# First batch: another order on VectorE and TensorE from the second scores on, and weights in pieces of 2, 2, 3, 2 and 3 blocks

## Chip, cores and metric

The kernel runs on one core of a Trainium2 chip. The metric is the device time of one launch in microseconds, as a median of runs; the profile shows one execution of the same program.

## What is computed

For q, k and v of shape (8 batches, 8 heads, 576 positions, 64), heads 0 to 3 attend to the last 32 positions and heads 4 to 7 to every 32nd position. The attention output, as 4608 tokens of 512 channels, goes through a bilinear feed-forward network with 1536 hidden channels.

```python
mask_local = (rel >= 0) & (rel < 32)
mask_strided = (rel >= 0) & (pos[None, :] % 32 == pos[:, None] % 32)
attn = softmax(where(mask, q @ k.T / 8, -1e9))
x = (attn @ v).transpose(0, 2, 1, 3).reshape(4608, 512)
out = ((x @ w_a) * (x @ w_b)) @ w_out
```

Inputs and output are float32; the kernel casts to bf16 while it loads.

## The kernel before, in words

**Stages.** Attention of batch 0 is done first, in a prologue. Then the feed-forward network runs in nine stages of 512 tokens, each with 12 hidden blocks of 128 (`ffn_ab`) and four output steps (`ffn_y`, L768). The attention of the batches 1 to 7 is spread between these stages' steps (the tables `STEPS` and `LATER`). All instructions are issued under a manual schedule: each engine works in the order in which the program names them.

**Units of attention.** A head pair c (0 and 1 local, 2 and 3 strided) has two halves, so a batch has eight units u = 0 to 7 with c = u // 2. In the prologue these are single steps, named in the string `ORDER`:

- `Tkcp`, `Tqcp`: transposes of keys or queries of pair c on TensorE (L287, L290, L296) into a PSUM buffer `tp`, of which there are two, used in turn; `Tkce` (VectorE, L307) and `Tqce` (ScalarE, L311) copy them out.
- `Sup`: scores on TensorE into `st`, of which there is one (L379, L385); `Sux`: exp on ScalarE (L393); `Sum`: the mask as a bitwise and on VectorE (L403), for local units only. Strided units of batch 0 get their mask from a matmul inside `Sup` (L379).
- `Vup`: p times v on TensorE (L442, L444) into `o`, of which there are two; `Vur`, `Vun`: reciprocal and normalization on VectorE (L450, L465).
- `Xcp`, `Xce`: the normalized output is transposed on TensorE (L511) and copied to `xT` on ScalarE (L523). `Xcp` takes a `tp` buffer too.
- `*n`: n filler matmuls of 224 columns (`spin`, L154), whose result nobody reads.
- `C0`, `C1`: casts of the first pieces that came as float32 (L834, L838). `M` and `G0` to `G2` make the masks; `G2` is a small matmul (L149) and, on VectorE, `mask_s` (L150).
- `F0A` to `F1c`: the first two hidden blocks of the feed-forward network, in parts (L581). `Z` zeroes a query buffer on ScalarE.

**Weights.** `load_w(c)` (L252) brings the hidden blocks `WCH[c]` to `WCH[c+1] - 1` of w_a and of w_b, one transfer each, from float32 in HBM to bf16 in SBUF. A row that lies together is 128 columns for each block: 512, 768 or 1024 bytes of bf16 for two, three or four blocks. The calls stand in step `G1`, on GpSimd's queue, before and between the loads for batch 1 (`load_qk`, L197; `load_vs`, L238). `load_wo` (L255) follows later on the same queue, in four pieces of three blocks.

Of the kernel before, what the change touches and what calls it, by code (L numbers as in the profile page):

```python
# [22 lines left out]
PAD = 32  # L23
PW = 344
VW = 128
WCH = (0, 2, 5, 9, 12)
FAST_Y = (2, 3, 4, 5, 6, 7, 8)


# [1 line left out]
def kernel(  # L31
# [81 lines left out]
    def zero_qz(i, eng, parts=((0, 0), (0, 1), (1, 0), (1, 1))):  # L113
        for j, z in parts:
            t = qz_buf[i][j][z]
            if (i, j, z) == (0, 0, 0):
                t = t[:, 1]
            if eng is nc.scalar:
                nc.scalar.copy(t, spare[:, :1].unsqueeze(2).to_broadcast(list(t.shape)))
            else:  # L120
                eng.memset(t, 0.0)
# [8 lines left out]
    def mask_local2():  # L130
        nc.vector.tensor_copy(mask_l, msl.unsqueeze(1).to_broadcast([128, 4, LW]))

        nc.vector.memset(mask_l[:PAD, 0], 0)
# [4 lines left out]
    def mask_group(part):  # L138

        if part == 0:  # L140
            nc.scalar.copy(by4(nm_l[lo, :NP]), ident[lo, :NP // 4].unsqueeze(2).to_broadcast([32, NP // 4, 4]))
            nc.scalar.copy(by4(nm_l[up, :NP]), ident[up, 32:36].unsqueeze(1).to_broadcast([32, NP // 4, 4]))
            nc.scalar.copy(nm_l[64:], nm_l[:64])
        elif part == 1:
            nc.vector.tensor_scalar(nm_r[up], nm_l[up, :NP], 1.0, 8e9, op0=ALU.subtract, op1=ALU.mult)
            nc.vector.tensor_copy(nm_r[64:], nm_r[:64])
        else:
            mp = cur["misc"][:NP, 256:256 + NP]
            nc.tensor.matmul(mp, lhsT=nm_l[:, :NP], rhs=nm_r, start=True, stop=True)  # L149
            nc.vector.tensor_scalar(mask_s, mp, 0.0, -1.0, op0=ALU.is_equal, op1=ALU.mult)  # L150

    def spin(n):
        for _ in range(n):
            nc.tensor.matmul(cur["misc"][:, :224], lhsT=nc.const_aps.tensor(1.0, [128, 128], BF16),  # L154
                             rhs=nc.const_aps.tensor(1.0, [128, 224], BF16), start=True, stop=True)
# [31 lines left out]
    def load_qk(b, strided, heads=range(HL), names="kq"):  # L187
        for nm in names:
            src = {"k": k, "q": q}[nm]
            if b < FIRST_D:  # L190
                n, R, h0 = (NP, RS, HL) if strided else (96, RL, 0)
                w0 = {"k6": 0, "q6": 1536, "k8": 3072, "q8": 5120}[f"{nm}{R}"]
                if b not in shared:
                    shared[b] = nat.tile([128, FG * 5 * SW], BF16, tag="shared", name="shared")
                t = nats[b, nm, strided] = shared[b][:n, w0:w0 + HL * R * D].rearrange("p (h r d) -> p h r d", r=R, d=D)
                hs = slice(heads[0], heads[-1] + 1)
                nc.gpsimd.dma_start(out=t[:, hs], in_=src[b, h0:h0 + HL].rearrange("h (p r) d -> p h r d", r=R)[:, hs])  # L197
            elif strided:

                t = nat_s[nm]  # L200
                n = 32 if b == FIRST_D else YS
                for h in heads:
                    nc.gpsimd.dma_start(
                        out=t[32 * h:32 * h + n],
                        in_=bass.AP(tensor=src.tensor, offset=(b * H + HL + h) * S * D,
                                    ap=[[RS * D, n], [YS * RS * D, 3], [1, RS * D]]))
            else:
                if 0 in heads:
                    nats[b, nm, strided] = nat.tile([128, NY, D], BF16, tag=f"{nm}l", name=f"{nm}l")
                t = nats[b, nm, strided]  # L210
                for h in heads:
                    nc.gpsimd.dma_start(out=t[32 * h:32 * h + 32],  # L212
                                        in_=src[b, h].rearrange("(i y) d -> y i d", y=32))
            nats[b, nm, strided] = t
# [18 lines left out]
    def load_vs(b, heads=range(HL)):  # L233
        if b < FIRST_D:

            for z in range(2):
                t = blocks("k", z)
                nc.gpsimd.dma_start(out=t[:NP, :, :RS * D],  # L238
                                    in_=v[b, HL + 2 * z:HL + 2 * z + 2].rearrange("h (p r) d -> p h (r d)", r=RS))
                nats[b, "v", z] = t  # L240
            return
        for h in heads:
            nc.gpsimd.dma_start(out=vs_buf[b % 2][:, h, :, 0:D],  # L243
                                in_=v[b, HL + h].rearrange("(p r) d -> p r d", r=RS))
# [4 lines left out]
    def load_w(c):  # L249
        f = slice(128 * WCH[c], 128 * WCH[c + 1])  # L250
        for src, dst in ((moe_w_a, wa_sb), (moe_w_b, wb_sb)):
            nc.gpsimd.dma_start(out=dst[:, :, f], in_=src.rearrange("(ko ki) f -> ki ko f", ki=128)[:, :, f])  # L252
# [13 lines left out]
    def by_row(t):  # L266
        return t.rearrange("p (r h d) -> p h r d", h=2, d=D)
# [257 lines left out]
    def step_X(b, c):  # L525
# [6 lines left out]
            "Xp": lambda c: X_p(0, c), "Xe": lambda c: X_e(0, c)}  # L532

    ORDER = """
        G0 C0 Tk0p *2 Tq0p Tk0e Tq0e *5 Tk1p S1p M G1 Tq1p S1x Tk1e *4 Tq1e S0p S1m *7 G2 C1 S0x S3p Tk2p Tq2p Tk2e S3x Tq2e *3
        S2p S2x V1p S0m *2 V1r S3m V0p V0r V1n V0n *2 S4p Tk3p Tk3e S2m Tq3p S4x Tq3e *2 S5p S5x X0p X0e *3 V2p V2r V3p V2n
        V3r V3n S6p V4p V4r V4n S6x X1p V5p V5r S7p X1e V5n V6p S7x F0A V6r V7p V6n X2p X2e Z F1A F0B V7r V7n F1B X3p F0b X3e
        F1b F0c F1c""".split()


    STEPS = {1: {5.5: "Tk2", 6: "Tq2", 7: "S4 Tk3", 7.5: "S5", 8: "Tq3", 8.5: "V4", 9: "S6 V5 Pk0", 9.5: "S7 Pq0",
# [30 lines left out]
    def ab_mm(t, f, ab, kks, mid=None, first=0, last=KD - 1, ws=(0, 1)):  # L572
        n = min(TTOK, XR * S - TTOK * t % (XR * S))
        cuts = [(0, n)] + ([(n, TTOK - n)] if n < TTOK else [])
        for w, ps_ in [((wa_sb, wb_sb)[i], ab[i]) for i in ws]:
            if mid and ps_ is ab[1]:
                mid()
            for kk in kks:
                for c0, n in cuts:
                    x0 = (TTOK * t + c0) % (XR * S)  # L580
                    nc.tensor.matmul(ps_[:, c0:c0 + n], lhsT=w[:, kk, 128 * f:128 * (f + 1)], rhs=xT[:, kk, x0:x0 + n],  # L581
                                     start=(kk == first and c0 == 0), stop=(kk == last and c0 == cuts[-1][0]))
# [214 lines left out]
    with tc.manual_schedule(engines={ENG.PE, ENG.SP, ENG.Pool, ENG.DVE, ENG.Activation}):  # L797
# [30 lines left out]
        for nm in ORDER:  # L828
            if nm[0] == "*":
                spin(int(nm[1:]))  # L830
            elif nm == "C0":
                for x, cp, n in ((raw[0], nc.vector.tensor_copy, "k"), (raw[1], nc.scalar.copy, "q")):
                    t = nats[0, n, False][:, 0:2].rearrange("p h r d -> p (h r d)")
                    cp(by_row(t), x[:96].rearrange("p (h r d) -> p h r d", h=2, d=D))  # L834
                    paired[0, n, 0] = t.rearrange("p (r m) -> p r m", r=RL)
            elif nm == "C1":
                for p in (slice(PAD, 64), slice(64, 128)):
                    nc.vector.tensor_copy(vl_buf[0][p, 0, 0:D], raw[2][p, :D])  # L838
            elif nm == "M":
                mask_local2()  # L840
            elif nm[0] == "G":
                mask_group(int(nm[1]))
                if nm == "G1":
                    load_vs(0)
                    for c in range(2):
                        load_w(c)
                    load_w(2)
                    load_qk(1, True, (0, 1))
                    load_qk(1, True, (2, 3))
                    load_vs(1)  # L850
                    load_w(3)
                    load_qk(1, False)
            elif nm == "Z":
                zero_qz(1, nc.scalar, ((0, 0),))
            elif nm[0] == "F":
                f = int(nm[1])
                if nm[2] == "A":
                    if f == 1:
                        ab = pst.tile([128, 2, 512], F32, tag="st", name="ab")
                        first[f] = [ab[:, 0], ab[:, 1]]  # L860
                    else:
                        first[f] = [psum4["misc"].tile([128, 512], F32, tag="misc", name="ab")]
                elif nm == "F0B":
                    first[f].append(psum4["o"].tile([128, 512], F32, tag="o", name="ab"))
                ab_mm(0, f, first[f], {"A": (0, 1), "B": (0, 1), "b": (2,), "c": (3,)}[nm[2]],
                      ws={"A": (0,), "B": (1,)}.get(nm[2], (0, 1)))
            else:
                PART[nm[:-2] + nm[-1]](int(nm[-2]))
# [101 lines left out]
```

## Time and profile before

| | |
|---|---|
| median of 6 runs | 328.82 us (328.54 to 329.35) |
| profiled execution | 328.54 us, of which the span is 326.4 |
| TensorE busy | 319.5 us, 98% of the span |
| VectorE, ScalarE, GpSimd busy | 81%, 62%, 54% |
| granted TensorE clock | 1.00 throughout |
| DMA | 37.50 MB in 98869 packets; software queue 64.4% of 16 engines' span |

The span is the time from the first to the last instruction. An engine's busy share is an average over the whole span; where a stage differs, the chain of waits, the timeline and the windows show it. In the software queue's figures several packets overlap on one DMA engine, so a share can pass 100% within a window. Start times are microseconds from the start of the span.

### The profile page before, as it was taken

What the parts mean: (1) busy time and instruction counts of PE and PEld (TensorE: products, weight loads), DVE (VectorE), ACT (ScalarE), POOL (GpSimd) and SP (SyncE); (2) the same over time, 40 slices, a digit from 0 to 9 for tenths busy, and PEclk for the clock granted to TensorE, in tenths of its full rate; (3) what the DMA queues carried; (4) which work ended last, traced back from release to release, by engine and by line L of the source; (5) the groups of instructions that cost most, each with busy time, mean ns of one, the idle gap of its engine ahead of it and who ended that gap; (6) DMA issues with size and microseconds to landing.
All of it is one profiled execution on the core that took longest, in us unless ns stands there. A gap on an engine that the chain in (4) does not pass through costs nothing.

```text
span 326.4 us, 7644 instructions
## 1 busy us (share of the span) xinstructions
PE 319.5 (98%) x2788; PEld 206.1 (63%) x2820; DVE 265.7 (81%) x509; ACT 202.3 (62%) x329; POOL 177.0 (54%) x295
## 2 busy tenths in 40 slices
PE   8999999999999999999999999999999999999995
PEld 6754655455555587557999985569555954584474
DVE  6766888889778999999999999999877845647562
ACT  6764775478777765777677757775677643313321
POOL 8935838699866555875577557753312031232021
PEclk9999999999999999999999999999999999999999
DMA  9999999999999798799979999898024022004004
GB/s 154 151 203 201 203 185 190 161 177 134 134 207 122 91 100 78 76 222 120 84 73 190 147 86 76 152 189 84 20 63 129 2 67 64 0 2 129 1 2 129
DMA packets 98869, 37.50 MB, mean 115 GB/s; under 512 B 76688, under 2 KB 96016, under 8 KB 98832
## 3 DMA queue, kind: packets, MB, share of 16 engines
q0 software_dynamic: 85968, 19.48, 64.4%
q1 hardware_dynamic: 12576, 17.34, 18.3%
q8 instruction: 22, 0.36, 0.5%
q10 hardware_dynamic: 288, 0.20, 0.2%
q14 instruction: 15, 0.12, 0.1%
HBM read 39.51 MB, written 9.44 MB: 150 GB/s over the span
## 4 chain that ended last, share of the span: by engine, by line
PE 91%; DVE 3%; issue 2%; DMA 2%; POOL 1%; ACT 1%; POOLq 0%; DVEq 0%; ACTq 0%
PE mm L581 51%; PE mm L686 16%; PE mm L768 6%; PE st L385 4%; PE o L486 4%; PE misc L154 2%; DMA kl<-in_k_dram 2%; PE mm L714 2%; PE o L442 1%; PE ab L581 1%; PE tp L511 1%; PE tp L287 1%; PE end L714 1%; DVE xT L500 1%; PE tp L296 1%
## 5 line engine op out<-in xcount | busy, mean ns | idle before, releaser
L581 PE MATMUL mm<-xT,wb_sb 128*128 128x512 bf16 (+1 forms) x465 | 109.1, 357 | 0.2
L581 PE MATMUL mm<-xT,wa_sb 128*128 128x512 bf16 (+1 forms) x451 | 108.2, 356 | 1.0
L598 ACT COPY a_sb<-mm 128x512 f32<-128x512 f32 x106 | 62.0, 585 | 48.4 <-PE mm L581 47.7
L936 POOL CAST pace<-pf 1x1 f32<-1x1 bf16 x84 | 31.3, 373 | 83.5 <-DVE pf L601 80.9
L581 PEld LDWEIGHTS <-wb_sb 128*128 128x128 bf16 x480 | 46.4, 98 | 44.0 <-issue 0.2
L601 DVE TENSOR_TENSOR pf<-a_sb,mm 128x512 bf16<-128x512 f32 x84 | 56.4, 672 | 17.0 <-PE mm L581 13.8
L581 PEld LDWEIGHTS <-wa_sb 128*128 128x128 bf16 x480 | 42.7, 98 | 31.2
L393 ACT ACTIVATE p<-st 128x576 bf16<-128x576 f32 (+1 forms) x64 | 41.5, 649 | 11.4 <-PE st L385 10.8
L495 ACT ACTIVATE xr<-o 64x576 f32<-64x576 f32 x48 | 31.1, 647 | 25.1 <-PE o L486 24.2
L686 PEld LDWEIGHTS <-ps 128*128 128x128 bf16 x360 | 34.6, 98 | 3.9
L496 ACT ACTIVATE xr<-xr 64x576 f32<-64x576 f32 x48 | 32.8, 683 | 1.5
L500 DVE TENSOR_TENSOR xT<-o,xr 64x288 bf16<-64x288 f32 x48 | 21.5, 448 | 7.4 <-ACT xr L496 6.7
L502 DVE TENSOR_TENSOR xT<-o,xr 64x288 bf16<-64x288 f32 x48 | 21.5, 448 | 6.4 <-ACT xr L496 5.1
L686 PE MATMUL mm<-wf,ps 128*128 128x256 bf16 x216 | 26.4, 273 | 0.0
L403 DVE TENSOR_TENSOR p<-p,mask_l 128x576 int16<-128x576 int16 x32 | 22.2, 693 | 1.2 <-ACT p L393 1.1
L768 PE MATMUL mm<-wo_sb,pf 128*128 128x512 bf16 x93 | 22.9, 379 | 0.1
L243 POOL DMA_DIRECT2D vs<-in_v_dram x24 | 19.6, 819 | 3.0 <-PE st L385 2.2
L212 POOL DMA_DIRECT2D kl<-in_k_dram x24 | 16.1, 670 | 5.4 <-issue 4.6
L212 POOL DMA_DIRECT2D ql<-in_q_dram x24 | 16.0, 666 | 5.3 <-DMA wo_sb<-in_moe_w_out_dram 4.1
L603 DVE TENSOR_TENSOR pf<-a_sb,mm 128x512 bf16<-128x512 f32 x22 | 14.9, 676 | 4.1 <-ACT a_sb L598 2.6
L936 POOL COPY pace<-y_sb 1x1 f32<-1x1 f32 x16 | 2.8, 175 | 27.9 <-ACT y_sb L669 15.1
L686 PE MATMUL mm<-wf,pf 128*128 128x256 bf16 x144 | 17.5, 273 | 0.0
(162 smaller groups left out, 503.2 us busy)
## 6 DMA issues: line engine op xcount, KB each, us to landing
out_dram<-y_sb SPq DMA_DIRECT2D x12, 512.0 KB, 5.2
out_dram<-y_sb SPq DMA_DIRECT2D x10, 256.0 KB, 3.6
vl<-in_v_dram POOLq DMA_DIRECT2D x6, 384.0 KB, 6.9
kl<-in_k_dram POOLq DMA_DIRECT2D x24, 72.0 KB, 3.2
ql<-in_q_dram POOLq DMA_DIRECT2D x24, 72.0 KB, 3.3
vs<-in_v_dram POOLq DMA_DIRECT2D x24, 72.0 KB, 3.9
wo_sb<-in_moe_w_out_dram POOLq DMA_DIRECT2D x4, 384.0 KB, 9.4
natk<-in_k_dram POOLq DMA_DIRECT2D x20, 72.0 KB, 3.4
```

Source lines behind the costliest of these rows:

```text
L212: nc.gpsimd.dma_start(out=t[32 * h:32 * h + 32], in_=src[b, h].rearrange("(i y) d -> y i d", y=32))
L393: nc.scalar.activation(p[:M, :, :W], st[:M, :, :W], ACT.Exp, scale=scale)
L403: nc.vector.tensor_tensor(pi, pi, mk, op=ALU.bitwise_and)
L495: nc.scalar.activation(r, sums, ACT.Ln)
L496: nc.scalar.activation(r, r, ACT.Exp, scale=-1.0)
L500: nc.vector.tensor_mul(dst[:, W * half:W * (half + 1)], o[:64, j, :W], r[:, j])
L581: nc.tensor.matmul(ps_[:, c0:c0 + n], lhsT=w[:, kk, 128 * f:128 * (f + 1)], rhs=xT[:, kk, x0:x0 + n], start=(kk == first and c0 == 0), sto ...
L598: nc.scalar.copy(a_sb, ab[0])
L601: nc.vector.tensor_mul(pf[:, f, :].rearrange("p (i a s) -> p a i s", i=2, s=16), halves(a_sb), halves(ab[1]))
L686: nc.tensor.matmul(bank[b][:, q], lhsT=lhs(g, q), rhs=rhs(g), start=new and q == 0 and g == 0, stop=g == FG - 1, skip_group_check=True)
L768: nc.tensor.matmul(ybank[j], lhsT=pf[:, f, 128 * j:128 * (j + 1)], rhs=wo_sb[:, f], start=(f == 0), stop=(f == FD - 1))
L936: nc.gpsimd.tensor_copy(pace, done)
```

## The change

Two things are changed together. In `ORDER`, from `G2 C1` on, steps are put in another place: `C1` before `G2`; `S3m`, `S2m` and `V0p` earlier; `V0r` after `V1n`; `S4x` and `S6x` right behind their scores; `Tk3e` after `V0n`; `X1p` behind `V5p`; `X2p` before `V7p`; and the fillers from `G2` on go from twelve to seven. The order on ScalarE stays as it was. `WCH` cuts the twelve blocks into 2, 2, 3, 2 and 3, where they were 2, 3, 4 and 3. The first nine blocks still precede the loads for batch 1, in eight transfers where there were six.

```diff
-WCH = (0, 2, 5, 9, 12)
+WCH = (0, 2, 4, 7, 9, 12)
...
-        G0 C0 Tk0p *2 Tq0p Tk0e Tq0e *5 Tk1p S1p M G1 Tq1p S1x Tk1e *4 Tq1e S0p S1m *7 G2 C1 S0x S3p Tk2p Tq2p Tk2e S3x Tq2e *3
-        S2p S2x V1p S0m *2 V1r S3m V0p V0r V1n V0n *2 S4p Tk3p Tk3e S2m Tq3p S4x Tq3e *2 S5p S5x X0p X0e *3 V2p V2r V3p V2n
-        V3r V3n S6p V4p V4r V4n S6x X1p V5p V5r S7p X1e V5n V6p S7x F0A V6r V7p V6n X2p X2e Z F1A F0B V7r V7n F1B X3p F0b X3e
-        F1b F0c F1c""".split()
+        G0 C0 Tk0p *2 Tq0p Tk0e Tq0e *5 Tk1p S1p M G1 Tq1p S1x Tk1e *4 Tq1e S0p S1m *7 C1 G2 S0x S3p Tk2p Tq2p Tk2e S3x Tq2e *2
+        S2p S2x V1p S0m S3m V1r V0p V1n V0r S2m V0n *2 S4p S4x Tk3p Tk3e Tq3p Tq3e *3 S5p S5x X0p X0e V2p V2r V3p V2n
+        V3r V3n S6p S6x V4p V4r V4n V5p V5r X1p X1e V5n S7p S7x V6p F0A V6r X2p X2e V7p V6n Z F1A F0B V7r V7n
+        F1B X3p F0b X3e F1b F0c F1c""".split()
...
                     load_w(2)
+                    load_w(3)
                     load_qk(1, True, (0, 1))
                     load_qk(1, True, (2, 3))
                     load_vs(1)
-                    load_w(3)
+                    load_w(4)
                     load_qk(1, False)
```

## The prediction

> **What bounds the kernel now.** The page's first part says that TensorE is the bound: 98% of the span, with 81% for the next engine. The page's chain agrees (PE 91% of it). The change touches only the first 23 us, so I then read the chain of waits from 5 to 45 us, to see what sets the moment at which TensorE turns into an unbroken stream of FFN matmuls.
>
> ```profile
> PE 319.5 (98%) x2788; PEld 206.1 (63%) x2820; DVE 265.7 (81%) x509; ACT 202.3 (62%) x329; POOL 177.0 (54%) x295
> ```
> ```profile
> 9.79 0.05 PE misc L149
> ...
> 9.86 0.23 DVE mask_s L150
> ...
> 10.12 0.18 DVE vl L838
> ...
> 10.32 0.44 DVE vl L838
> ...
> 10.79 0.46 DVE kT0s L307
> ...
> 11.28 0.47 DVE p L403
> ...
> 11.80 0.35 PE o L442 x6
> ...
> 14.25 0.29 PE misc L154 x3
> 14.54 0.20 PE o L442 x6
> ...
> 14.99 0.56 DVE xr L465
> ...
> 19.06 1.30 PE ab L581 x6
> ```
>
> The columns are start, duration, engine, tile and line. VectorE makes mask_s, casts the two pieces of v (C1), copies the keys (Tk2e), masks p (S0m); only then can V0p run on TensorE. From 16.2 us on every step of the chain is a TensorE one. A shift of F1A (the matmuls that stand at 18.89 us in the timeline) is a shift of the end, unless data come late.
>
> Data are the second bound. The DMA row of the page is at 9 in its first 13 slices: 105 us of queues that are hardly ever empty. GpSimd's queue carries all weights, so each landing is fixed by the bytes ahead of it. I took landing = issue (timeline of POOL) + microseconds to landing (DMA view of the window that holds one issue):
>
> ```profile
> shared<-in_k_dram POOLq DMA_DIRECT2D x1, 144.0 KB, 14.3
> ```
> ```profile
> wb_sb<-in_moe_w_b_dram POOLq DMA_DIRECT2D x1, 384.0 KB, 8.8
> ```
> ```profile
> wo_sb<-in_moe_w_out_dram POOLq DMA_DIRECT2D x1, 384.0 KB, 8.5
> ```
> ```profile
> 42.94 1.46 PE L768 MATMUL mm<-wo_sb,pf 128*128 128x512 bf16 x6
> ```
>
> They were issued at 15.31, 28.00 and 35.04 us, so they land at 29.6, 36.8 and 43.5. Batch 1's first transposes (Tk2) start at 30.01, the matmuls of block 9 on wb at 37.01, and the fourth of the six wo_sb matmuls at 42.94 + 3 x 0.216 = 43.59. The margins are 0.4, 0.2 and under 0.1 us. **TensorE runs dense here, but it arrives just when its data do.**
>
> **What the skill says.** The Trainium skill, "DMA: Bandwidth & Descriptors", section Why small descriptors are slow, gives each packet a fixed overhead. The trace agrees, in three windows whose packets are nearly all of one size (pieces of 2 blocks: 512 B, 3: 768 B, 4: 1024 B), at 16, 34.5 and 23 us:
>
> ```profile
> DMA packets 382, 0.19 MB, mean 191 GB/s; under 512 B 10, under 2 KB 382, under 8 KB 382
> ```
> ```profile
> DMA packets 411, 0.30 MB, mean 203 GB/s; under 512 B 15, under 2 KB 411, under 8 KB 411
> ```
> ```profile
> DMA packets 420, 0.41 MB, mean 207 GB/s; under 512 B 16, under 2 KB 420, under 8 KB 420
> ```
>
> The same page, section Why a DMA increments its semaphore by 16 and not by 1, says that all 16 engines must have finished before the data count as landed: one late engine delays a piece. No run here shows it by itself. "TensorE: Matmul & The Clock Gate", section What's actually happening, lets the clock fall only after an idle window of about 3.4 us. The trace has PEclk at 9 in all slices, and the gaps below are under 0.5 us, so dropping spins costs no clock.
>
> **The change, part by part.**
>
> *Head of the VectorE chain.* C1 now stands ahead of mask_s, where VectorE idles 0.79 us for the mask product. It runs from 9.05, and the key copy waits only for its own eight transposes: about 10.00 + 8 x 0.033 + 0.2 = 10.47, against 10.79. S0m and V0p follow 0.32 earlier, at 11.48.
>
> *Masks and copies reordered.* S3m now precedes V1r, S2m precedes V0n. With the spacings of the trace (reciprocal 0.22, normalization 0.49, mask 0.41 from start to start): V1n 11.99, S2m 12.57, V0n 12.98, Tk3e 13.45 to 13.9. Tk3e is 0.25 later than now.
>
> *Spins.* Twelve of these fillers become seven. The two ahead of S4p now end at 11.9, since V0p is earlier and no spins precede it; S4p then waits for the end of S2x (11.95) and starts at 12.0 instead of 12.28. S4x is at 12.5, S5p at 13.2.
>
> *The new wait.* X0p takes the transpose buffer of Tk3 (two buffers, order Tk2 Tq2 Tk3 Tq3 X0), so it waits for Tk3e: 13.95 against 13.82 now. Behind it stand V2p, V3p and S6p. The three spins after X0p are gone, so V2p still starts at 14.21 and not 14.38, and V2n and V3n come 0.17 earlier (V3n ends at 16.06).
>
> *X1 behind V5.* V5p waits for V3n until 16.12, and X1p now follows it: X1p 16.56, X1e on ScalarE 17.03 instead of 16.63. S7x is queued behind X1e on ScalarE: 17.6 instead of 17.46. V7p waits for S7x until 18.33; X2p, moved ahead of V7p, fills part of that gap. V7p ends at 18.77 and F1A starts there, against 18.89: **-0.12 us**. The lower end is the 0.32 of the first step; the upper is +0.1, if X1e's delay passes whole.
>
> *Weights.* Nine blocks go ahead of batch 1's loads in both kernels, in eight transfers for six. Of the bytes, 0.79 MB in 3-block and 1.05 MB in 4-block pieces (0.79/0.203 + 1.05/0.207 = 8.95 us) become 1.05 MB in 2-block and 0.79 MB in 3-block ones (1.05/0.191 + 0.79/0.203 = 9.37). All behind them in the queue lands **0.4 us later**. From below: the present 2-block pieces took about 1.3 us each, the 3-block ones 2.0 and the 4-block ones 2.6 by differences of landings, 9.2 before and 9.2 after: 0. From above: the packets' own durations counted without overlap, 1.2 us. I take 0.4; the windows measure exactly these sizes. Nothing is cheaper for a smaller piece arriving sooner: blocks 2 to 8 now land ahead of their use (wb of 5 to 8 at 27.7 for 28.28), and block 4, now in the third pair, lands near 25 for its use at 26.2.
>
> *GpSimd's queue.* Two more issues at 0.81 us are 1.6 us. Behind them stand batch 1's loads: the first moves from 15.31 to about 17. The issues already wait for the landing eight transfers back (0.58 on wa_sb, 0.71 and 1.83 on wb_sb), and over 5 us of bytes lie queued then. I cost this at nothing; the backlog hides it. SP's queue has nothing there.
>
> **The sum.** TensorE arrives 0.12 us earlier and the data 0.4 later. At Tk2 the keys land at 30.0 for 29.9: +0.05. At block 9, 37.2 for 37.0: +0.25. At wo_sb, 43.9 against 43.5, used at 43.59: +0.37. Behind that TensorE is dense, so nothing gives it back; the later loads hang on tokens that TensorE's results release and move along. The profiled execution (328.54 = span 326.4 + 2.1 outside it) becomes 328.9; the median stands 0.28 above it, so **329.2 us**. About 0.2% (0.66 us) is what a measurement can tell from no change.
>
> **Rivals.**
> A, the forecast: 328.9 to 329.6; it crosses the bound if the delay exceeds 0.7. Chance 0.50, of it 0.42 within 0.2% and 0.08 slower.
> B, packet size costs nothing: the head's 0.12 is caught by wo_sb's margin of under 0.1. 328.7. For it, the landing differences; against it, the three rates. 0.16, of it 0.15 within and 0.01 faster.
> C, **slower**: the packets' durations count whole, or a late engine of the 16 falls on a piece. The wait is at wo_sb's second piece, and beyond 0.7 us of DMA delay it decides: 1.2 - 0.06 = 1.1, 329.9 (to 330.6 with a straggler). For it, the margin of nothing; against it, a queue that shows 124 to 142% of overlap. 0.26.
> D, faster: the margin is not a data limit and the head gains more than replayed (the 0.32, plus the spins' 0.5): 328.0. Against it, the X1e and Tk3e waits. 0.08, of it 0.07 faster.
> That the change does nothing is excluded: the built instructions stand in the new order, with ten spin rows (five loads, five matmuls) fewer on TensorE and two transfers more on GpSimd.
>
> The sums are faster 0.08, within 0.58, slower 0.34. The range, 328.4 to 330.2, leaves out D and the end of C.
>
> **What would show it.** Right: the key copy near 10.5, X0p behind Tk3e, F1A at 18.6 to 18.9, batch 1's k landing near 30.0, and small TensorE waits at 30, 37 and 43.6. Wrong: wo_sb landing at 43.5 or sooner (B), beyond 44.3 (C), or F1A past 19.2, which would mean that a wait in the head was missed.

## The result: slower by 0.38%, by a falling TensorE clock

The changed kernel took 330.01 us in the median (35 runs, 328.15 to 332.62) against 328.82: a ratio of 1.0038, with an interval of 1.0023 to 1.0052. This ratio and those below are not quotients of the two medians, and they leave out runs over 1.5% above the fastest of the same kernel, which are the two slowest of `e7_before_no_fillers` and of `e9_order_fillers_s6`. The median hides what happened. The 36 executions with a clock on record fall into three groups by the clock that TensorE was granted over the whole execution:

| mean granted clock | executions | median us |
|---|---|---|
| 0.997 to 1.000 | 17 | 328.80 |
| 0.995 | 5 | 330.42 |
| 0.987 to 0.990 | 14 | 331.95 |

More than half of the executions lost clock. The rest are as fast as the kernel before. The profiled execution is of the third group: 332.12 us, span 330.4, clock 0.987. The page shows it in its clock row, with a 9 in every slice for the kernel before.

```profile
PE   8899999999999999999999999999999999999994
...
PEclk9959999999999999999999999999999999999999
```

One slice of 8.3 us, from about 16.5 to 24.8 us, has half the clock while the PE row above it still shows a busy engine. The trace's clock record gives the limits: half speed from 18.15 to 24.98 us, which is 6.83 us. (The record starts only at 4.50 us here and at 6.60 us in the profile before. Ahead of that the kernel before has 23 fillers in 4.45 us, 0.19 us each for 0.093 later: TensorE begins at half speed, which a clock of "1.00 throughout" does not count.) The windows view of the changed kernel, cut at these limits and at half that length, 3.41 us (columns: window, its length, then busy time and instruction count of PE, PEld, DVE, ACT and POOL; clock, DMA share, GB/s):

```profile
11.33:14.74 3.41, 2.64 (x54) 2.03 (x55) 2.24 (x7) 2.85 (x5) 3.10 (x5) 1.00 1.44 141
14.74:18.15 3.41, 2.95 (x77) 2.42 (x77) 2.89 (x8) 1.13 (x3) 2.52 (x4) 1.00 1.40 190
18.15:21.56 3.41, 3.17 (x44) 2.21 (x42) 1.94 (x5) 2.23 (x4) 1.77 (x3) 0.50 1.40 200
21.56:24.98 3.42, 3.42 (x16) 1.54 (x15) 0.08 (x1) 0.83 (x2) 1.35 (x2) 0.50 1.35 200
24.98:28.40 3.42, 3.37 (x17) 1.52 (x16) 2.10 (x4) 1.76 (x3) 1.44 (x2) 1.00 1.36 198
```

In the two windows ahead of the fall TensorE was busy for 2.64 and 2.95 of 3.41 us; it was never idle for long. The kernel before, in windows counted in the same way from the start of its own record, has 3.32 and 3.08 at about that time:

```profile
10.02:13.43 3.41, 3.32 (x72) 2.38 (x69) 3.29 (x11) 2.52 (x5) 3.41 (x6) 1.00 1.48 136
13.43:16.84 3.41, 3.08 (x80) 2.67 (x78) 2.55 (x8) 2.55 (x5) 3.20 (x5) 1.00 1.27 170
```

In the two at 0.50 it counts as busy almost throughout, but with few instructions: each follows the one before after twice the time. The chain of waits of the changed kernel (start, duration, what) shows the same six matmuls (F1A, F0B, F1B) that took 1.30 us before at 2.58, and the eight behind them at 2.42 us:

```profile
8.25 6.43 DMA vl<-in_v_dram
...
14.72 0.36 PE o L442 x6
...
18.24 0.66 ACT p L393
...
18.92 0.63 PE ab L581
...
20.65 2.58 PE ab L581 x6
...
23.71 2.42 PE ab L581 x8
```

The first block of the unbroken stream starts at 25.96 us instead of 22.24, 3.7 us late. At half clock, 6.83 us cost up to 3.4 us; from 26 us on TensorE is dense and gives nothing back.

The chain also names a wait that the profile before does not have: V2p stands ready and v's second half has not landed. In the waits view from 13 to 20 us:

```profile
PE o L442 <- DMA vl<-in_v_dram: 0.7, 1, 0.7
```

In the kernel before that load landed at 13.6 us and V2p started at 14.38. Here it landed at 14.7, and V2p, without fillers ahead of it, had nothing to do from 14.03 on.

### The profile page after: what moved, and what is told of

Same layout as the page of the kernel before. It is cut to its first block, busy times and chain, and to the rows that moved or that the text cites. A ratio compares the mean times of both kernels' runs of the same rounds, so it can differ in the third digit from the quotient of the medians.

```text
span 330.4 us, 7636 instructions
## 1 busy us (share of the span) xinstructions
PE 321.6 (97%) x2783; PEld 206.7 (63%) x2815; DVE 265.9 (80%) x509; ACT 202.4 (61%) x329; POOL 178.3 (54%) x297
## 4 chain that ended last, share of the span: by engine, by line
PE 92%; POOL 2%; DMA 2%; issue 1%; DVE 1%; ACT 0%; POOLq 0%; DVEq 0%
PE mm L581 55%; PE mm L686 17%; PE mm L768 6%; PE st L385 4%; PE o L486 4%; DMA vl<-in_v_dram 2%; PE ab L581 2%; PE mm L714 2%; POOL shared L197 1%; PE o L442 1%; PE tp L511 1%; PE end L714 1%; POOL vl L225 0%; DVE xr L465 0%; PE tp L287 0%
## 5 line engine op out<-in xcount | busy, mean ns | idle before, releaser
L495 ACT ACTIVATE xr<-o 64x576 f32<-64x576 f32 x48 | 31.1, 647 | 25.1 <-PE o L486 24.8
```

Of the source, the lines that this page charges most:

```text
L495: nc.scalar.activation(r, sums, ACT.Ln)
```

## The experiments

Three theories. **Clock**: the new order has fewer fillers and new waits between 13 and 18 us; TensorE is then too little active and its clock halves for one window of 3.41 us or two, each worth about half its length. **Pieces**: smaller packets make all later loads land later, and TensorE waits for them (the prediction's own term). **New waits**: the order lengthens the head chain by itself. An execution is called dropped below if its mean granted clock is under 0.997; one window at half clock is worth 0.5 x 3.41 / 327 = 0.005. The kernel before, run beside the experiments, was dropped in 6 of 75, 2 of 51 and 3 of 59 executions, and took 328.9 us at full clock. These are three groups on three chips (the versions e1 to e4, e5 to e8, e9 to e12). The kernel before drops seldom on each, so the chip alone does not make the difference.

### Each half of the change alone

`e1_order_only`: the new `ORDER`, with the old pieces; its edit against the changed kernel:

```diff
-WCH = (0, 2, 4, 7, 9, 12)
+WCH = (0, 2, 5, 9, 12)
...
-                    load_w(3)
                     load_qk(1, True, (0, 1))
...
-                    load_w(4)
+                    load_w(3)
```

> The new ORDER with the old weight pieces (2, 3, 4, 3 blocks). Clock theory: the loss comes from TensorE's clock, which halves for one or two windows of 3.4 us where the prologue has fewer fillers and more waits; the order alone carries it, so about half of the executions show a mean granted clock under 0.997 and times 1.7 or 3.4 us above the rest, median 329.5 to 331. Pieces theory (smaller packets make later loads land later): 328.6 to 328.9 and clock 1.0 throughout.

Measured: 329.79 us (22 runs), ratio 1.0029 (1.0006 to 1.0051). 11 of 22 dropped: four at 330.3, seven at 331.9. At full clock the median is 328.63. The order carries the loss. At full clock it is no slower than the kernel before: 0.3 us below by the medians, 0.2 by the means, which eleven executions do not tell from nothing.

`e2_pieces_only`: the old `ORDER` with the new pieces; its edit against the kernel before:

```diff
-WCH = (0, 2, 5, 9, 12)
+WCH = (0, 2, 4, 7, 9, 12)
...
+                    load_w(3)
                     load_qk(1, True, (0, 1))
...
-                    load_w(3)
+                    load_w(4)
```

> The old ORDER with the new weight pieces (2, 2, 3, 2, 3 blocks). Clock theory: as the kernel before, 328.7 to 329.0, with the clock under 0.997 in no more than one execution in ten. Pieces theory: 329.2 to 330.0 at a clock of 1.0.

Measured: 329.21 us, ratio 1.0006 (0.9990 to 1.0022); 4 of 22 dropped, more than was expected of the clock theory (one in ten) but few enough to leave open whether the pieces add anything there. At full clock 329.03, 0.1 above the kernel before. Its waits view from 25 to 45 us does show the wait that the prediction named, at block 9's wb:

```profile
PE mm L581 <- DMA wb_sb<-in_moe_w_b_dram: 0.2, 1, 0.2
```

### Fillers put in and taken out

`e3_after_fillers3`: the changed kernel with the three fillers back ahead of V2p.

```diff
-X0p X0e V2p V2r
+X0p X0e *3 V2p V2r
```

> The changed kernel with three fillers put back between X0p and V2p, nothing else. Clock theory: 0.28 us more of TensorE activity in the window around 14 to 18 us makes clock drops rarer than in the changed kernel (under a quarter of executions), median 328.6 to 329.3. Theory of new waits (X0p behind Tk3e, X1e behind V5p): fillers cure nothing, 330 as the changed kernel. Pieces theory: 330 too.

Measured: 329.21 us, ratio 1.0014 (0.9996 to 1.0031); 8 of 22 dropped, six of them for one window only. Against 19 of 36 the count is too close to decide; the shorter drops (two of eight for two windows, against 14 of 19) and the median lean to the clock theory. The expected quarter was missed: three fillers are not enough.

`e4_before_no_fillers3`: the opposite edit in the kernel before.

```diff
-X0p X0e *3 V2p V2r
+X0p X0e V2p V2r
```

> The kernel before without the three fillers between X0p and V2p, nothing else. Clock theory: the clock drops in a third or more of the executions, each costing 1.7 or 3.4 us, and the median goes to 329.2 or above. Theory of new waits and pieces theory: V2p starts up to 0.3 us earlier, so 328.5 to 328.8.

Measured: 8 of 22 dropped, against 6 of 75 beside it, which chance hardly explains; ratio 1.0025 (1.0003 to 1.0047). The median, 329.10, stays just short of what was expected, since 14 runs kept their clock (328.91). Removing 0.28 us of useless matmuls makes the kernel slower.

`e7_before_no_fillers`: the kernel before without any of the twelve fillers behind `G2`.

```diff
-Tq2e *3 S2p
+Tq2e S2p
...
-S0m *2 V1r
+S0m V1r
...
-V0n *2 S4p
+V0n S4p
...
-Tq3e *2 S5p
+Tq3e S5p
...
-X0e *3 V2p
+X0e V2p
```

> The kernel before without any of the twelve fillers behind G2. Clock theory: drops in over two thirds of the executions, often for two windows, median 331 to 332, though the executions at full clock take 328.5 to 328.9. Rivals: fillers only cost time, so 328.3 to 328.8 throughout.

Measured: 330.01 us, ratio 1.0029 (1.0004 to 1.0054). 8 of 22 dropped, all for two windows or more, 332.65 in the median. Over two thirds and a median of 331 to 332 were expected, so this was missed: it is no more often than without three, and the count isn't proportional to the fillers. At full clock it takes 329.30, so not even there did leaving them out save time. In its profiled execution (330.16 us, clock 1.00) TensorE waits 0.5 us for wb and 1.1 us for VectorE's xT, waits that the profile before does not have; whether they are usual, these runs don't show.

`e5_before_fillers_s6`: three fillers *more* in the kernel before, in a gap of 0.33 us behind S6p.

```diff
-V3r V3n S6p V4p
+V3r V3n S6p *3 V4p
```

> The kernel before with three fillers more, between S6p and V4p, where TensorE stands idle for 0.33 us. Clock theory: clock drops, in 8% of the executions of the kernel before, become rarer still (none to one in 22), median 328.7 to 329.0. Pieces or new-wait theory: no change at all in how often, median 328.8 to 329.1.

Measured: none of 14 dropped; 328.88 us, ratio 1.0003 (0.9991 to 1.0015). It fits, but shows little: at 6% a drop, 14 executions without one have a chance of about 0.4.

`e8_after_fillers`: the changed kernel with fillers in both gaps.

```diff
-X0p X0e V2p V2r
+X0p X0e *5 V2p V2r
...
-S6p S6x V4p
+S6p S6x *4 V4p
```

> The changed kernel with five fillers before V2p and four before V4p. Clock theory: drops in under 10% of executions, median 328.7 to 329.1. Pieces theory or new-wait theory: 330 with drops as often as in the changed kernel (19 of 36). If the smaller pieces cost something at full clock, it stays 0.1 to 0.3 us above the same idea with the old pieces.

Measured: none of 14 dropped; 329.12 us, ratio 1.0005 (0.9996 to 1.0015). Against 19 of 36, nine fillers take the drops away: order and pieces are as changed.

`e11_after_fillers_early`: the control, with three fillers where TensorE has hardly a gap.

```diff
-S0p S1m *7 C1 G2
+S0p S1m *10 C1 G2
```

> A control: the changed kernel with three fillers put to the seven ahead of C1, about 9.5 us, where TensorE has hardly a gap. Clock theory: activity between 13 and 18 us is not raised, so the clock drops about as often as in the changed kernel (a third to two thirds of executions), median 329.5 to 331. If it is the number of fillers alone that counts: drops under a quarter, median 328.9 to 329.2.

Measured: 11 of 22 dropped, 329.74 us, ratio 1.0023 (1.0001 to 1.0045). As the changed kernel: three fillers in this place cure nothing that can be told. But three ahead of V2p alone (8 of 22 in `e3_after_fillers3`) are not told apart from that either, and five to nine early ones were not tried. **Place and number are therefore not separated.** Number alone would sort all versions, those below included. With twelve or more fillers from `G2` on, the kernel before dropped in 11 of 185, `e2_pieces_only` in 4 of 22 and five versions in none of 14 each. With ten or fewer, the three early ones counted in, every version dropped in 5 to 11 of 22, and the changed kernel in 19 of 36.

The windows view from 13.5 to 17.0 us, for the kernel before, the changed kernel, the order alone, `e5_before_fillers_s6`, `e10_order_fillers_2_3` (below) and `e11_after_fillers_early`, in this order (second number after the window: TensorE busy):

```profile
13.50:17.00 3.50, 3.17 (x82) 2.76 (x83) 2.64 (x8) 2.64 (x5) 3.13 (x5) 1.00 1.28 172
```
```profile
13.50:17.00 3.50, 2.27 (x55) 1.82 (x52) 1.88 (x7) 1.88 (x4) 2.55 (x5) 1.00 1.27 171
```
```profile
13.50:17.00 3.50, 2.47 (x61) 2.00 (x60) 1.99 (x6) 1.86 (x4) 3.04 (x5) 1.00 1.35 174
```
```profile
13.50:17.00 3.50, 3.47 (x82) 2.83 (x78) 2.45 (x8) 2.45 (x5) 2.81 (x4) 1.00 1.30 175
```
```profile
13.50:17.00 3.50, 2.78 (x60) 2.14 (x59) 1.61 (x6) 2.17 (x4) 2.13 (x4) 1.00 1.35 181
```
```profile
13.50:17.00 3.50, 2.99 (x76) 2.52 (x76) 2.67 (x9) 2.19 (x4) 2.87 (x4) 1.00 1.31 175
```

For the first four, 3.17, 2.27, 2.47 and 3.47 of 3.50 us busy go with 11 of 185, 19 of 36, 11 of 22 and 0 of 14 executions dropped. The last two don't fit: 2.78 goes with 0 of 14, and 2.99 with 11 of 22. The busy time of one execution in this stretch does not sort the versions. All but the changed kernel's are profiles of executions that kept their clock, and with the same program that is a matter of chance.

### Fillers with the new order, and the pieces with the clock held

`e6_order_fillers`: order alone, three fillers in each gap.

```diff
-X0p X0e V2p V2r
+X0p X0e *3 V2p V2r
...
-S6p S6x V4p
+S6p S6x *3 V4p
```

> New ORDER, old weight pieces, three fillers before V2p and three before V4p. Clock theory: drops in under 15% of executions (order alone: 11 of 22), and the level at full clock stays at the order's 328.6, so the median is 328.5 to 328.9, the fastest of all. Theory that the order's own waits cost time: 329.5 and drops as often as with the order alone.

Measured: none of 14 dropped, 329.13 us, ratio 1.0008 (0.9998 to 1.0019). The clock holds, but the expected 328.5 to 328.9 was missed: the level at full clock is 0.5 above that of the order alone, which suggests that fillers ahead of V2p are paid for.

`e9_order_fillers_s6`: only the three ahead of V4p. `e10_order_fillers_2_3`: two ahead of V2p besides.

```diff
-S6p S6x V4p
+S6p S6x *3 V4p
```

> New ORDER, old pieces, three fillers between S6p and V4p alone, where TensorE waits for V2n anyway. Clock theory: drops in under a quarter of executions (11 of 22 without them); no cost at full clock, so the level stays at 328.6 and the median is 328.6 to 328.9. If fillers delay what follows, the level at full clock is 328.9 to 329.2.

Measured: 5 of 22 dropped, 328.57 at full clock, median 328.71 against 329.00 beside it. The ratio, 1.0005 (0.9986 to 1.0024), takes in three of the five drops and shows no gain.

```diff
-X0p X0e V2p V2r
+X0p X0e *2 V2p V2r
```

> As the one before, with two fillers more between X0p and V2p, where TensorE waits for v's second half. Clock theory: drops in under 10%, median 328.7 to 329.0. If fillers there delay V2p, the level at full clock is near the 329.1 of the version with three and three.

Measured: none of 14 dropped, 329.01 us, ratio 0.9994 (0.9975 to 1.0014). Steady, and not faster than the kernel before. No version here is shown to beat it.

`e12_pieces_fillers_s6`: old order, new pieces, three fillers ahead of V4p.

```diff
-V3r V3n S6p V4p
+V3r V3n S6p *3 V4p
```

> Old ORDER, new pieces, three fillers between S6p and V4p: against the same with the old pieces (328.88) it shows what the pieces cost with the clock held. Clock theory says nothing on it. Pieces theory: loads behind the weights land 0.3 to 0.4 us later and TensorE waits for them, 329.1 to 329.3. Landing differences theory (pieces cost nothing): 328.8 to 328.95.

Measured: none of 14 dropped, 328.79 us against 328.88 with the old pieces, ratio to the kernel before 0.9991 (0.9969 to 1.0013). At a steady clock the pieces cost nothing that can be told in the time of a launch. Yet the landings did move. From the landing of wa's first piece to that of wo_sb's second the traces show 26.1 us in the mean of eight profiles with the old pieces (25.8 to 26.6) and 26.6 in six with the new (26.3 to 26.8).

## Why the prediction was right in its range and wrong in its reason

The range held 330.01 by luck. The likeliest time, 329.2 and within 0.2%, did not come true, and the slower case that had the right size (C: 329.9) was to come from late packets, which isn't what happened.

**The step that failed** is the sentence "The trace has PEclk at 9 in all slices, and the gaps below are under 0.5 us, so dropping spins costs no clock." The Trainium skill ("TensorE: Matmul & The Clock Gate", What's actually happening) speaks of an idle window of about 3.4 us. The window's length is what the trace shows: half clock lasted 6.83 us, twice 3.41. But the engine need not be idle in it. The clock fell after two windows with 2.64 and 2.95 us of busy time and no gap over 0.7 us. Where page and measurement differ, the measurement decides. And dropping fillers did cost clock: without three of them the kernel before dropped in 8 of 22 executions instead of 6 of 75. I had the fillers' cost (0.093 us each) in the sum and took their use for nothing.

**Head of the VectorE chain**, -0.12: the first step came, the gain at its end did not. In the timeline of VectorE in the changed kernel the key copy starts at 10.33, for the 10.47 replayed and 10.79 before, and C1 does stand ahead of it, at 9.01.

```profile
9.01 0.53 DVE L838 CAST vl<-raw 32x64 bf16<-32x64 f32 x2
9.72 0.23 DVE L150 TENSOR_SCALAR mask_s<-misc 72x72 int16<-72x72 f32 x1 [0.18 <-PE misc L149]
10.33 0.46 DVE L307 COPY kT0s<-tp 128x576 bf16<-128x576 bf16 x1 [0.38 <-PE tp L296]
```

Behind it the new order is the slower one. V2p and F1A in TensorE's timeline, of the kernel before and then of `e3_after_fillers3`, which has the new order and kept its clock:

```profile
14.38 0.53 PE L442 MATMUL o<-vl,p 128*128 128x65 bf16 x12
...
18.89 0.60 PE L581 MATMUL ab<-xT,wa_sb 128*128 128x512 bf16 x2
```
```profile
14.02 0.53 PE L442 MATMUL o<-vl,p 128*128 128x65 bf16 x12
...
18.84 0.59 PE L581 MATMUL ab<-xT,wa_sb 128*128 128x512 bf16 x2
```

The stretch from V2p to F1A takes 4.79 to 4.82 us in all seven full-clock profiles with the new order and 4.51 to 4.66 in the six with the old; the replay had 4.56 (14.21 to 18.77). With X1e ahead of it on ScalarE, S7x starts 3.49 to 3.52 us after V2p, for 3.39 replayed and 3.08 before. So F1A starts at 18.84 at best, for 18.89, and past 19.2 in four of the seven profiles, the prediction's own sign of a missed wait. The medians at full clock with the order alone (328.63, and 328.57 with fillers ahead of V4p, for 328.9) have no such gain to rest on; by the means they are 0.2 and 0.1 below.

**A wait that was missed.** V2p was replayed against VectorE alone. With the masks done earlier and the fillers gone, v's second half became the last to come. The changed kernel's profile has 0.7 us of it. That load landed between 13.6 and 15.2 us in the fourteen profiles, and V2p waited for it in six, two of them with the old order. The wait lengthens the stretch ahead of the fall; how large its share in the drops is was not tried.

**Pieces**: later landings by 0.4 were predicted from the packet rates, and 0.46 was measured. The step from there to the end, +0.37 through wo_sb, isn't seen in the time: `e12_pieces_fillers_s6` and `e5_before_fillers_s6` differ by -0.1, the changed kernel and its order alone, both at full clock, by +0.17 (328.80 and 328.63). Part of the reason is a term that the sum took as fixed, the 2.1 us outside the span. At full clock it is 1.70 to 1.72 us in the mean in all six versions with the new pieces, and 2.14 to 2.16 in all eight with the old, so these gain 0.4 us there. Their spans are longer, by the medians 327.05 for 326.75 us in the first pair and 327.10 for 326.50 in the second. But 0.3 of that arises after 95 us, far behind wo_sb: from VectorE's first multiplication of line 601 to the end of the span it is 231.9 us in all six profiles with the new pieces and 231.6 in all eight with the old. An estimate from these figures leaves 0 to 0.3 us for the later landings. Why the other two shifts go with the pieces stays open. The margins were read from one execution, to within 0.1 us, while landings move by more than that between executions. The wait exists (0.2 at block 9 in `e2_pieces_only`), but not as a shift in every execution.

**GpSimd's two issues**, costed at nothing: batch 1's first load was issued at 17.86 instead of 15.31 and its data landed at 29.3, for 29.6 before. The backlog hid it.

The sum that the runs support: at full clock 328.80, not told apart from the kernel before; on top of it the drops, with 5 of 36 executions at +1.6 and 14 at +3.1, which lift the mean by about 1.4 us and the median by 1.2.

## What to carry to other kernels

A filler on TensorE can have a use that no wait shows: here it made drops of the clock rarer. Before one is removed, or work is moved so that a dense stretch gets thin, price a possible loss at half of one or two windows with a chance, and measure the chance over many executions: one profile's busy time did not tell it. When a kernel's executions spread more than before, sort them by granted clock before reading a median: here the sorted groups showed a change that cost nothing that can be told at full clock and lost by chance events. And compare spans as well as times: what lies outside the span moved by 0.4 us here.

## What was not expected of the hardware

- In the clock records of the fourteen profiles every complete stretch is a whole number of windows of 3.41 us: 4, 94 or 95 at full clock, 2 at half. The drops of the other executions fit this: in groups of four executions or more, one costs 1.2 to 1.6 us here, and two (a mean clock of 0.987 to 0.990) 2.9 to 3.4. The kernel before has them too, in 11 of 185 executions.
- The level of activity at which the clock falls isn't settled. In windows counted from the start of each record, six profiles have one or two with TensorE busy for only 0.73 to 0.80 of them and kept the clock; in the changed kernel's it was lost after 0.77 and 0.86. The record starts between 3.6 and 6.6 us in these executions, so the phase of the windows against the program differs and may decide; so may how many rows and columns the matmuls fill. Neither was tried.
- A load's landing varied by 1.6 us between profiles (v's second half, 13.6 to 15.2 us), far more than the margins of 0.1 to 0.4 that the prediction leaned on.
